# Down products of a transformer block by seven matrix products instead of eight, with three row operands kept in DRAM

## The chip, the core and the metric

The kernel runs on one core of a Trainium2 chip. The metric is the device time of one execution in microseconds (us). The core has five engines that run their own queues of instructions in order and wait for each other through semaphores: TensorE (PE, matrix products into PSUM), VectorE (DVE), ScalarE (ACT), GpSimd (POOL) and SyncE (SP, which here issues DMA transfers).

## The reference

The reference is one transformer block on 2048 rows of width 576 in float32: layer norm, attention with 32 heads, a residual, then a second layer norm and a gated feed-forward with 4608 inner columns.

```python
x = A_x
h = x + _A_ref(_layernorm(x), A_wqkv, A_wo)          # attention
def _B_ref(x, w_gate, w_up, w_down):
    g = einsum("bsd,df->bsf", x, w_gate)
    u = einsum("bsd,df->bsf", x, w_up)
    return einsum("bsf,fd->bsd", gelu(g) * u, w_down)
h2 = h + _B_ref(_layernorm(h), B_w_gate, B_w_up, B_w_down)
```

The change lies in the last product, gelu(g) * u times w_down, called the down product here.

## The kernel before

Matrices are cut into a high and a low float16 part, and a product is made of high-high, high-low and low-high parts, three matmuls where one float32 product would be one.

The feed-forward runs over 18 chunks of 256 inner columns. Two chunks make a super chunk (nine of them, the loop over `sc`, L1289). The rows lie in two halves of 1024 (`p` = 0 and 1), each of two blocks of 512. For a chunk and a half, `unit(c, p)` (L1051) makes gate and up products by a Strassen scheme of Winograd's form: seven products for gate and seven for up, in turn, each of seven matmuls of 128x512 (L1065) that accumulate in a bank. There are six banks, g[0..2] for gate and u[0..2] for up. The operands of the rows are 35 pieces (five for each of B22, B11, B21, T1, T2, T3, T4); 18 of each half lie in the region X and 17 in the region V. After each product, elementwise work follows: ACT copies a bank (`copy`), DVE adds another bank to the copy, ACT takes the gelu (L1070), DVE multiplies by the up value (`gate`, L1073), ACT writes the high float16 part of the result (`high`, L1076) and POOL the low part (`low`, L1079). A unit gives four blocks of h: two row blocks by two column blocks of 128.

After the two chunks of a super chunk, `down(p)` (L1142) makes the down product for that half: for 8 row tiles of 128 and 2 column halves of 288, twelve matmuls of 128x288 (L300) into one of four banks in turn, and then one DVE instruction (L1155) that adds the bank, scaled, into the rows `nat`. So a down has 16 groups of 12 matmuls.

The order in a super chunk is: unit(c, 1), unit(c+1, 1), down(1), unit(c+2, 0), unit(c+3, 0), down(0), where the last three belong to the next super chunk. The order on PE, ACT, DVE, POOL and SP is that of the program text. Beside the main work runs `side`, a chain of generators that cuts the next chunks' weights: one step of it is taken after each product of a unit and each group of a down (`beside`, L1265). `split_matrix` (L927) has steps for sums of weight blocks on POOL (L936), maxima on DVE (L129), a transpose on PE, a run of six tiny DVE instructions (L142 to L173) that make the scale, and then three highs on ACT (L952: one of 1152 columns, two of 768) and three lows on DVE (L966 and L968). `split_down` (L1021) cuts the down weights in the same way, with four highs and four lows of 576 columns. Weights come by DMA on SP's queue into one buffer in the region A.

Of the lines in the listing below, the prediction's steps use `unit`, `down`, `split_matrix`, `split_down` and the loop over `sc`.

## Time and profile before

| what | before |
|---|---|
| median of 3 runs | 2670.18 us (2669.16 to 2671.85) |
| the profiled execution's own time | 2668.08 us |
| its span, first to last instruction | 2666.3 us |
| mean granted TensorE clock | 0.996 of full speed |
| first matmul of the feed-forward (L1065) | at 1449.2 us of the span |
| PE busy, whole span | 97% |
| DVE busy, whole span | 76% |
| ACT, POOL busy | 61%, 29% |

The page gives busy time, a span in 40 slices, DMA queues, the chain of work that ended last, and groups of instructions by line. A wait is shown as idle time of the engine ahead of an instruction, with what released it. In the timeline each row has start, duration, engine, line, and in brackets the idle time before it.

### The profile page before, as it was taken

How to read it: one execution, taken by the hardware profiler on the slowest of the kernel's cores; microseconds unless marked ns; L12 is line 12 of the kernel's file. 1: busy time of each engine (PE TensorE's matmuls, PEld its weight loads, DVE VectorE, ACT ScalarE, POOL GpSimd, SP SyncE). 2: the span in 40 equal slices, each digit the busy share in tenths (PEclk: the TensorE clock that was granted, in tenths of full speed). 3: DMA queues.
4: the chain of work that ended last, by engine and by line, in shares of the span. 5: the costliest groups of instructions: out<-in, count | busy, mean ns of one | idle time of the engine just before them, and what ended most of it. 6: DMA issues, size and time to landing. Idle time of an engine off the chain costs nothing.

```text
span 2666.3 us, 44517 instructions
## 1 busy us (share of the span) xinstructions
PE 2589.7 (97%) x16665; PEld 1118.6 (42%) x16665; DVE 2013.1 (76%) x3872; ACT 1619.2 (61%) x2128; POOL 777.3 (29%) x1040
## 2 busy tenths in 40 slices
PE   6999999999999999999999899999999999999999
PEld 2542222222222222222243555555555555555555
DVE  6367999999999999999967866566666666666653
ACT  5215999999999999999956433333333333333332
POOL 2200352132223232221666532222222222222221
PEclk9999999999999999999999999999999999999999
DMA  8411101010101010110116321010101010101010
GB/s 222 94 40 51 54 26 30 19 42 15 42 14 45 17 42 19 30 25 20 36 47 125 74 51 40 23 40 23 40 22 40 24 39 25 38 27 36 29 59 36
DMA packets 171466, 114.70 MB, mean 43 GB/s; under 512 B 90872, under 2 KB 149772, under 8 KB 171250
## 3 DMA queue, kind: packets, MB, share of 16 engines
q1 hardware_dynamic: 163566, 99.06, 13.9%
q0 software_dynamic: 7552, 12.79, 1.8%
q8 instruction: 130, 2.13, 0.3%
q14 instruction: 86, 0.70, 0.1%
q10 hardware_dynamic: 132, 0.01, 0.0%
HBM read 76.51 MB, written 15.01 MB: 34 GB/s over the span
## 4 chain that ended last, share of the span: by engine, by line
PE 67%; ACT 15%; issue 7%; DVE 4%; POOL 2%; DMA 2%; SPq 0%; ACTq 0%; DVEq 0%; POOLq 0%
PE more L1065 14%; PE bank L1065 13%; ACT WK L644 10%; PE bank L300 10%; PE bank L648 9%; PE more L300 8%; PE bank L589 7%; PE pair L300 4%; ACT nat L595 4%; PE pair L642 2%; DVE mx L601 1%; DMA nat<-rc 1%; ACT nat L662 0%; POOL A L996 0%; DMA V<-V 0%
## 5 line engine op out<-in xcount | busy, mean ns | idle before, releaser
L644 ACT ACTIVATE WK<-pair 128x1024 f32<-128x1024 f32 x1024 | 1000.0, 1041 | 84.8 <-PE pair L642 84.1
L601 DVE TENSOR_REDUCE mx<-bank 128x1 f32<-128x512 f32 x1552 | 975.7, 683 | 42.8 <-PE bank L589 32.4
L648 PE MATMUL bank<-WK,V 128*32 128x512 f32 x4096 | 547.7, 606 | 0.2 <-ACT nat L662 0.2
L300 PEld LDWEIGHTS <-WK 128*128 128x128 f16 x3456 | 338.0, 98 | 90.9 <-ACT WK L1076 1.7
L1065 PEld LDWEIGHTS <-W 128*128 128x128 f16 x2394 | 234.3, 98 | 282.9 <-issue 5.7
L589 PE MATMUL bank<-W 54*128 54x512 f16 x896 | 258.2, 379 | 14.0 <-DVE mx L601 1.8
L589 PE MATMUL bank<-A 54*128 54x512 f16 x904 | 255.0, 380 | 16.8 <-DVE mx L601 5.3
L671 POOL TENSOR_TENSOR rp<-rc,minus_one 128x16 f32<-128x16 f32 x28 | 81.9, 2926 | 537.1 <-DMA rc<-nat 537.1
L300 PE MATMUL more<-W,WK 128*128 128x288 f16 x1728 | 235.6, 286 | 2.2 <-ACT WK L1076 1.4
L300 PE MATMUL bank<-W,WK 128*128 128x288 f16 x1728 | 235.2, 286 | 0.0
L1065 PE MATMUL bank<-X,W 128*128 128x512 f16 x792 | 223.8, 379 | 0.0
L642 PE MATMUL pair<-A 56*128 56x512 f16 x1024 | 212.9, 381 | 2.3 <-ACT WK L644 1.4
L642 PE MATMUL pair<-W 56*128 56x512 f16 x1024 | 210.3, 380 | 4.3 <-ACT WK L644 3.2
L1065 PE MATMUL bank<-V,W 128*128 128x512 f16 x720 | 202.4, 379 | 0.4 <-ACT tmp L1115 0.3
L936 POOL TENSOR_TENSOR A<-A 128x384 f32<-128x384 f32 x136 | 137.0, 1028 | 202.6 <-DMA A<-in_B_w_up_dram 118.7
L589 PEld LDWEIGHTS <-W 54*128 54x128 f16 x1024 | 75.1, 93 | 283.6 <-issue 266.6
L599 DVE CUSTOM_DVE_ANT_0 nat<-bank,nat 128x512 f32<-128x512 f32 x248 | 171.4, 691 | 27.1 <-PE pair L642 4.4
L589 PEld LDWEIGHTS <-A 54*128 54x128 f16 x1024 | 72.3, 93 | 267.9 <-issue 250.8
L1079 POOL TENSOR_TENSOR WK<-tmp,WK 128x512 f16<-128x512 f32 x73 | 87.9, 1203 | 305.9 <-ACT WK L1076 305.6
L1083 ACT COPY tmp<-more 128x512 f32<-128x512 f32 x36 | 21.0, 583 | 236.8 <-PE more L1065 198.2
L595 ACT ACTIVATE nat<-bank 128x512 f32<-128x512 f32 x248 | 151.4, 611 | 11.5 <-PE bank L589 11.5
L648 PEld LDWEIGHTS bank<-WK,V 128*32 128x32 f32 x4096 | 81.1, 108 | 179.0 <-issue 164.2
(304 smaller groups left out, 3259.9 us busy)
## 6 DMA issues: line engine op xcount, KB each, us to landing
A<-in_B_w_down_dram SPq DMA_DIRECT2D x8, 1152.0 KB
nat<-rc SPq DMA_DIRECT2D x32, 256.0 KB
A<-in_B_w_gate_dram SPq DMA_DIRECT2D x64, 128.0 KB
A<-in_B_w_up_dram SPq DMA_DIRECT2D x64, 128.0 KB
qk_hi<-tmp SPq DMA_DIRECT2D x36, 128.0 KB
qk_lo<-tmp SPq DMA_DIRECT2D x36, 128.0 KB
out_dram<-nat SPq DMA_DIRECT2D x16, 288.0 KB
X<-nat SPq DMA_DIRECT2D x100, 36.0 KB
```

The lines of the kernel that those rows point to most:

```text
L300: nc.tensor.matmul(dst, a, b, start=(i == 0), stop=(i == len(pairs) - 1))
L589: nc.tensor.matmul(pm[:, :TB], Q[r, q0 : q0 + P], keys, start=True, stop=True)
L595: nc.scalar.activation(row, pm[:, :TB], AF.Relu)
L599: nc.vector.tensor_tensor_reduce(row, pm[:, :TB], row, 1.0, LOWEST, ALU.add, ALU.max, dst)
L601: nc.vector.tensor_reduce(dst, pm[:, :TB], axis=AX.X, op=ALU.max)
L642: nc.tensor.matmul(pS[:, j, :TB], K[r, kt * P : (kt + 1) * P], Q[r, qc * TB : (qc + 1) * TB], start=True, stop=True)
L644: nc.scalar.activation(pes[(2 * kt + pr) % NPE], pS[:, :, :TB], AF.Exp, scale=ex_reg)
L648: nc.tensor.matmul(acc[32 * hh : 32 * hh + 32, :TB], Vg[n // NB][:, kt * G4 + hh * VC : kt * G4 + hh * VC + 32], pes[(2 * kt + hh // 2) % ...
L671: nc.gpsimd.tensor_tensor(rc, den, minus_one.to_broadcast([P, R]), op=ALU.pow)
L936: op(W8[:, d], W8[:, a], W8[:, b])
L1065: nc.tensor.matmul(bank, w, x_, start=start and i == 0, stop=i == len(mm) - 1, skip_group_check=not start)
L1079: nc.gpsimd.tensor_sub(hl[:, 2 * i + j], v, hh[:, 2 * i + j])
```

## The change

From the second super chunk on, the down product is made by the same Winograd form of Strassen's scheme: the four blocks of h and the four blocks of the down weights are combined into seven pairs, so `down7` runs 2 x 7 x 2 = 28 groups of six matmuls of 128x288, 168 in place of 192, and each group is followed by one DVE addition into `nat` (28 in place of 16). One bank may be accumulated into again by a later product after DVE has read it, as `b0` is by groups 1, 3, 5 and 7 of a pass, where a group now stands for two tiles i.

`unit7` takes the place of `unit` from chunk 2 on. It makes the products in another order (the pair S4 B22 ahead of A22 T4), and forms H1 to H4 from the four blocks of h. That makes four more DVE instructions with both inputs in SBUF (L1185, L1192, L1198, L1204), seven highs in place of four on ACT (L1130) and seven lows in place of four on POOL (L1133).

`split_down7` makes the seven combinations of the down weights: eight POOL instructions of 128x288, four highs (864, 1152, 864, 1152 columns) on ACT and four lows of the same sizes on DVE.

The larger buffers for h take the space of the pieces of the second half of the rows. So T2, T3 and T4 of both halves (15 pieces, 128x7680 float16) are written once to DRAM (`keep_pieces`, two transfers of 1.97 MB on ACT's queue), and from then on fetched into one place in V before they are needed (`fetch_pieces`: three transfers of 128x2560 float16, 655 KB, for each change of p, on SP's queue, issued in the unit that used that place last, `used`).

```diff
-    V = const.tile([P, 9936], F32, name="V")
+    V = const.tile([P, 10224], F32, name="V")
...
+    xs = [dram.tile([P, 15, TB], F16, name=f"xs{i}") for i in range(2)]
+
+    def piece(p, k, c):
 
         if k < 18:
             o = (2 * p + k // 9) * TB
             return XT[:, k % 9, o : o + TB]
-        return VP[:, p * PIECES + k - 18]
+        return VP[:, (p * PIECES if k < 20 or c < 2 else 0) + k - 18]
+
+    def keep_pieces(p):
+        nc.scalar.dma_start(xs[p], VP[:, p * PIECES + 2 : (p + 1) * PIECES])
+
+    def fetch_pieces(p, o):
+        nc.sync.dma_start(VP[:, 2 + 5 * o : 7 + 5 * o], xs[p][:, 5 * o : 5 * o + 5])
...
+    D11, D3, D21, D22, D1, D2, D4 = range(7)
+    dh7 = view(W, 23296, (2, 7, HALF), F16)
+    dl7 = [view(W, 31360, (7, HALF), F16), view(V, 36864, (7, HALF), F16)]
+    hts7 = [[view(r, o + 14 * TB * k, (7, TB), F16) for k in range(2)] for r, o in ((WK, 0), (V, 19456))]
...
+    def split_down7(sc):
+
+        raw = view(A, DS + 3 * 4 * HALF, (4, D))
+        T1, T2, T4 = (view(A, DS + 4 * HALF * i, (HALF,)) for i in range(3))
+        t124 = view(A, DS, (3, HALF))
+        ed = yield from exponents([raw[:, 2 * i : 2 * i + 2].rearrange("p a b -> p (a b)").unsqueeze(1)
+                                   for i in range(2)], "dn")
+        E = small.tile([P, 2], I32, tag="E", name="E")
+        nc.vector.tensor_add(E, ee[:, 0], ee[:, 1])
+        nc.vector.tensor_add(ed, ed, E)
+        M = small.tile([P, 1], I32, tag="M", name="M")
+        nc.vector.tensor_max(M, ed[:, 0:1], ed[:, 1:2])
+        nc.vector.tensor_sub(E, E, M.to_broadcast([P, 2]))
+        nc.vector.tensor_scalar(E, E, 1, 266, op0=ALU.mult, op1=ALU.add)
+        nc.vector.tensor_scalar_max(E, E, 0)
+        s = pow2(E, 1, 0, "s_dn")
+        dscs.append(pow2(M, 1, -259, "dsc"))
+
+        def sums(k):
+            B11, B12, B21, B22 = (raw[:, 2 * k + i // 2, i % 2 * HALF : (i % 2 + 1) * HALF] for i in range(4))
+            nc.gpsimd.tensor_sub(T1, B12, B11)
+            nc.gpsimd.tensor_sub(T2, B22, T1)
+            nc.gpsimd.tensor_sub(T4, B21, T2)
+            nc.gpsimd.tensor_sub(B12, B22, B12)
...
+        def high(j):
+            k, sl, src = jobs[j]
+            nc.scalar.activation(dh7[:, k, sl], src, AF.Copy, scale=s[:, k : k + 1])
+
+        def low(j):
+            k, sl, src = jobs[j]
+            nc.vector.scalar_tensor_tensor(dl7[k][:, sl], src, s[:, k : k + 1], dh7[:, k, sl],
+                                           op0=ALU.mult, op1=ALU.subtract)
+
+        sums(0)
+        yield
+        high(0)
+        yield
+        low(0)
+        high(1)
+        sums(1)
+        yield
+        low(1)
+        high(2)
+        yield
+        low(2)
+        high(3)
+        yield
+        low(3)
+        yield
+        blank_rows()
...
+    def unit7(product, gelu, gate, g, u, hh, hl, used):
...
+        xg, xu = next(tmp_ring), next(tmp_ring)
+        product(0, g[0], A11, B11, True)
+        nc.scalar.copy(xg, g[0])
+        yield
+        product(1, u[0], A11, B11, True)
+        nc.scalar.copy(xu, u[0])
+        yield
+        product(0, g[1], A12, B21, True)
+        nc.vector.tensor_add(xg, g[1], xg)
+        yield
+        product(1, u[1], A12, B21, True)
+        gelu(xg, xg)
+        nc.vector.tensor_add(xu, u[1], xu)
+        gate(xg, xu)
+        yield
+        ag, au = next(tmp_ring), next(tmp_ring)
+        product(0, g[0], S2, T2, False)
+        nc.scalar.copy(ag, g[0])
+        high(H11, xg)
+        yield
+        product(1, u[0], S2, T2, False)
+        used(0)
+        nc.scalar.copy(au, u[0])
+        low(H11, xg)
+        yield
+        bg, bu = next(tmp_ring), next(tmp_ring)
+        product(0, g[2], S1, T1, True)
+        nc.scalar.copy(bg, g[2])
+        yield
+        product(1, u[2], S1, T1, True)
+        nc.scalar.copy(bu, u[2])
+        yield
+        product(0, g[0], S3, T3, False)
+        nc.vector.tensor_add(bg, g[0], bg)
+        yield
+        product(1, u[0], S3, T3, False)
+        used(1)
+        gelu(bg, bg)
+        nc.vector.tensor_add(bu, u[0], bu)
+        gate(bg, bu)
+        yield
+        product(0, g[2], S4, B22, False)
+        nc.vector.tensor_add(ag, g[2], ag)
+        high(H22, bg)
+        gelu(ag, ag)
+        yield
+        product(1, u[2], S4, B22, False)
+        low(H22, bg)
+        nc.vector.tensor_add(au, u[2], au)
+        gate(ag, au)
+        nc.vector.tensor_add(xu, ag, bg)
+        yield
+        ga = next(tmp_ring)
+        product(0, g[0], A22, T4, False)
+        high(H1, xu)
+        gelu(ga, g[0])
+        low(H1, xu)
+        nc.vector.tensor_sub(bu, xu, xg)
+        high(H2, bu)
+        low(H2, bu)
+        yield
+        product(1, u[0], A22, T4, False)
+        used(2)
+        nc.vector.tensor_sub(au, xg, ag)
+        gate(ga, u[0])
+        high(H12, ga)
+        low(H12, ga)
+        high(H3, au)
+        low(H3, au)
+        nc.vector.tensor_sub(bg, ga, bu)
+        high(H4, bg)
+        low(H4, bg)
...
+        if c >= 2:
+            yield from unit7(product, gelu, gate, g, u, hh7, hl7, used or (lambda o: None))
+            return
...
+    def down7(p, dsc, last):
+
+        b0, b1, b2 = ((banks[i], banks[i + 3]) for i in (1, 0, 2))
+
+        def product(i, bank, a, b, start):
+            tsl = slice(i * P, (i + 1) * P)
+            mm = []
+            for k in range(2):
+                hh, hl = (v[:, a, tsl] for v in hts7[k])
+                mm += [(hh, dh7[:, k, b]), (hh, dl7[k][:, b]), (hl, dh7[:, k, b])]
+            for n, (w, x_) in enumerate(mm):
+                nc.tensor.matmul(bank[:, :HALF], w, x_, start=start and n == 0, stop=n == len(mm) - 1,
+                                 skip_group_check=not start)
+
+        def add(i, bank, *outs):
+            for j, n in outs:
+                t = (2 * p + j) * TPB + i
+                ws = slice(n * HALF, (n + 1) * HALF)
+                nc.vector.scalar_tensor_tensor(nat[:, t, ws], bank[:, :HALF], dsc, nat[:, t, ws],
+                                               op0=ALU.mult, op1=ALU.add)
+
+        for i0 in (0, 2):
+            for bank, a, b, start, outs in ((b0, H11, D11, True, ((0, 0),)),
+                                            (b2, H1, D1, True, ((1, 1),)),
+                                            (b0, H2, D2, False, ((0, 1),)),
+                                            (b1, H12, D21, True, ((0, 0),)),
+                                            (b0, H3, D3, False, ((1, 1),)),
+                                            (b2, H4, D22, False, ((0, 1),)),
+                                            (b0, H22, D4, False, ((1, 0),))):
+                for i in range(2):
+                    product(i0 + i, bank[i], a, b, start)
+                    add(i0 + i, bank[i], *outs)
+                yield
+            if last:
+                for i in range(2):
+                    for j in range(2):
+                        t = (2 * p + j) * TPB + i0 + i
+                        nc.sync.dma_start(ov[:, t], nat[:, t])
+            b0, b1 = b1, b0
+        banks[:] = [banks[i] for i in (1, 0, 2, 4, 3, 5)]
...
-                      split_matrix(c + 3, 1, None, lambda sc=sc: load_down(sc + 1), 2))
-            dn = split_down(sc + 1)
+                      split_matrix(c + 3, 1, None, lambda sc=sc: load_down7(sc + 1), 2))
+            dn = split_down7(sc + 1)
             side = chain(until_ready(g2))
+        if sc == 0:
+            keep_pieces(0)
         beside(unit(c, 1), side, head=0 if sc else 7)
         run(side)
+        if sc == 0:
+            keep_pieces(1)
         if not last:
             side = chain(g2, pause(2), u2, pause(2), g3, pause(2), u3, pause(4), dn)
-        beside(islice(u := unit(c + 1, 1), 13), side)
+        beside(islice(u := unit(c + 1, 1, None if last else lambda o: fetch_pieces(0, o)), 13), side)
         run(u)
-        beside(down(1, dsc, last), side, head=2)
+        beside(down7(1, dsc, last) if sc else down(1, dsc, last), side, head=2)
         if last:
             break
+        if sc == 0:
+            tmps[5] = view(WK, 14336, (TB,))
         run(u2)
         beside(unit(c + 2, 0), side)
         run(u3)
-        beside(unit(c + 3, 0), side)
+        beside(unit(c + 3, 0, lambda o: fetch_pieces(1, o)), side)
         run(dn)
         if sc + 2 < NCH // 2:
             load_matrix(w_gate, c + 4)
-        beside(down(0, dscs[-1], sc == NCH // 2 - 2), iter(()))
+        beside(down7(0, dscs[-1], sc == NCH // 2 - 2), iter(()))
     in_order.close()
 
 
```

Three places show how the rows stand. The first is DVE's queue at the end of the second unit of p = 1, ahead of down(1). Before (L1132 and L1136 add banks, L966 and L968 are lows of the next up weights, L1073 is the gate, L1155 the first additions of the down):

```order
L1132 TENSOR_TENSOR WK<-more_12981,WK 128x512
L966 SCALAR_TENSOR_TENSOR WK<-A,p_s_m_20846,W 128x768
L968 SCALAR_TENSOR_TENSOR W<-A,p_s_m_20846,W 32x3x128
L1136 TENSOR_TENSOR W<-bank_68,W 128x512
L1073 SCALAR_TENSOR_TENSOR WK<-W,p_hsc_20014,WK 128x512
L1155 SCALAR_TENSOR_TENSOR nat<-more_12979,p_dsc,nat 128x288
L1155 SCALAR_TENSOR_TENSOR nat<-bank_66,p_dsc,nat 128x288
L1155 SCALAR_TENSOR_TENSOR nat<-more_12980,p_dsc,nat 128x288
```

Now (L1183 adds a bank, L1185, L1192, L1198 and L1204 are the new sums, L978 and L980 the lows, L1342 the additions of the down; six tiny instructions that end in L173 are shown by the last one):

```order
L1183 TENSOR_TENSOR WK<-bank_68,WK 128x512
L1232 SCALAR_TENSOR_TENSOR WK<-WK,p_hsc_17880 128x512
L1185 TENSOR_TENSOR V<-WK,A 128x512
...
L173 TENSOR_SCALAR p_s_m_18728<-pi_s_m_18726 128x1
L1192 TENSOR_TENSOR tmp_81<-V,tmp_81 128x512
L978 SCALAR_TENSOR_TENSOR WK<-A,p_s_m_18728,W 128x768
L980 SCALAR_TENSOR_TENSOR W<-A,p_s_m_18728,W 32x3x128
L1198 TENSOR_TENSOR WK<-tmp_81,WK 128x512
L1232 SCALAR_TENSOR_TENSOR tmp_81<-bank_67,p_hsc_17880,tmp_81 128x512
L1204 TENSOR_TENSOR A<-tmp_81 128x512
L1342 SCALAR_TENSOR_TENSOR nat<-more_12981,p_dsc,nat 128x288
L1342 SCALAR_TENSOR_TENSOR nat<-bank_66,p_dsc,nat 128x288
```

The tiny instructions, which stood before the last bank additions, and four new sums now stand between the bank addition L1183 and the first addition of the down.

The second is ACT's queue at the end of the first unit of p = 0, ahead of the second. Before (L952 highs of weights, L1111 and L1115 copies, L1070 gelu, L1076 highs of h, L1083 the first copy of the next unit):

```order
L952 ACTIVATE W<-A,p_s_m_18971 128x1152
L952 ACTIVATE W<-A,p_s_m_18971 128x768
L1111 COPY A<-more_12979 128x512
L952 ACTIVATE W<-A,p_s_m_18971 128x768
L1115 COPY tmp_81<-bank_66 128x512
L1070 ACTIVATE A<-A,p_gsc_18515 128x512
L1070 ACTIVATE tmp_81<-more_12979,p_gsc_18515 128x512
L1076 CAST WK<-A 128x512
L1076 CAST WK<-tmp_81 128x512
L1070 ACTIVATE WK<-WK,p_gsc_18515 128x512
L1076 CAST WK<-WK 128x512
L1083 COPY tmp_81<-more_12979 128x512
```

Now (L964 highs of weights, L1229 gelu, L1130 highs of h; the gelu that reads the bank `more_12981` is the last of the four):

```order
L964 ACTIVATE W<-A,p_s_m_19112 128x1152
L1229 ACTIVATE A<-A,p_gsc_18638 128x512
L964 ACTIVATE W<-A,p_s_m_19112 128x768
L1130 CAST WK<-A 128x512
L1229 ACTIVATE WK<-WK,p_gsc_18638 128x512
L964 ACTIVATE W<-A,p_s_m_19112 128x768
L1130 CAST WK<-V 128x512
L1229 ACTIVATE tmp_81<-more_12981,p_gsc_18638 128x512
L1130 CAST WK<-tmp_81 128x512 x2
L1130 CAST WK<-WK 128x512
L1130 CAST WK<-A 128x512
L1137 COPY tmp_81<-more_12981 128x512
```

The highs of the weights moved in between the gelus, and the gelu that reads the bank of g[0] now comes behind a high of a new sum (L1130 WK<-V).

The third is DVE's queue at the end of the second unit of p = 0, ahead of down(0). Before (L1041 lows of the down weights):

```order
L1073 SCALAR_TENSOR_TENSOR A<-tmp_81,p_hsc_20014,A 128x512
L1041 SCALAR_TENSOR_TENSOR W<-A,p_s_dn,W 128x576
L1073 SCALAR_TENSOR_TENSOR tmp_81<-bank_66,p_hsc_20014,tmp_81 128x512
L1132 TENSOR_TENSOR WK<-more_12981,WK 128x512
L1136 TENSOR_TENSOR W<-bank_68,W 128x512
L1073 SCALAR_TENSOR_TENSOR WK<-W,p_hsc_20014,WK 128x512
L1155 SCALAR_TENSOR_TENSOR nat<-more_12979,p_dsc,nat 128x288
L1155 SCALAR_TENSOR_TENSOR nat<-bank_66,p_dsc,nat 128x288
```

Now (L1100 lows of the down weights, L1177 and L1183 bank additions):

```order
L1177 TENSOR_TENSOR WK<-more_12983,WK 128x512
L1100 SCALAR_TENSOR_TENSOR W<-A,p_s_dn,W 128x1152
L1183 TENSOR_TENSOR WK<-bank_68,WK 128x512
L1232 SCALAR_TENSOR_TENSOR WK<-WK,p_hsc_19032 128x512
L1185 TENSOR_TENSOR V<-WK,A 128x512
L1100 SCALAR_TENSOR_TENSOR V<-A,p_s_dn,W 128x864
L1192 TENSOR_TENSOR tmp_81<-V,tmp_81 128x512
L1100 SCALAR_TENSOR_TENSOR V<-A,p_s_dn,W 128x1152
L1198 TENSOR_TENSOR WK<-tmp_81,WK 128x512
L1232 SCALAR_TENSOR_TENSOR tmp_81<-bank_66,p_hsc_19032,tmp_81 128x512
L1204 TENSOR_TENSOR A<-tmp_81 128x512
L1342 SCALAR_TENSOR_TENSOR nat<-more_12982,p_dsc,nat 128x288
```

Before, the last low stood ahead of the last two bank additions (L1132, L1136). Now two of the four lows, each of half as many columns again or twice as many, stand behind the last one (L1183), among the new sums.

21 lines of the change are left out of this document (17 added, 4 removed).

## The prediction

> **What bounds the kernel now.** I read the chain of waits first, in a window that holds a whole super chunk, then the stages, then the timelines of DVE, ACT and POOL at the ends of units.
>
> ```profile
> PE 2589.7 (97%) x16665; PEld 1118.6 (42%) x16665; DVE 2013.1 (76%) x3872; ACT 1619.2 (61%) x2128; POOL 777.3 (29%) x1040
> ...
> 1909.95 1.51 PE bank L1065 x7
> 1911.46 1.47 PE more L300 x12
> ...
> 1933.51 1.47 PE bank L300 x12
> 1934.98 1.51 PE more L1065 x7
> ...
> 1977.51 1.47 PE more L300 x12
> ...
> 1911.46:1934.98 23.52, 23.52 (x194) 18.75 (x192) 9.13 (x17) 0.62 (x1) 5.39 (x6) 1.00 0.08 24
> 1911.46:2043.77 132.31, 132.31 (x785) 76.78 (x783) 82.71 (x160) 48.38 (x72) 35.90 (x34) 1.00 0.11 32
> ```
>
> Through units and downs the chain is PE alone, without a gap: a product of a unit takes 1.51 us, twelve matmuls of a down 1.47, a down 16 x 1.47 = 23.52 (first window row), a super chunk 132.31 (second). After the core's own time stand busy PE, PEld, DVE, ACT, POOL: DVE has 82.71 of 132.31. So removed matmuls are worth their full time, but only while the other engines deliver at the ends of units.
>
> **What is removed.** A down has 168 matmuls in place of 192: 24 x 1.47 / 12 = 2.94 us. Sixteen downs are changed (p = 1 of super chunks 2 to 9, p = 0 the same): 47.0 us off PE.
>
> **What is added.** Per super chunk DVE gets 24 more additions and 16 sums, ACT and POOL twelve highs and lows and the wider cuts of the down weights. In total that fits: 24 x 0.44 + 16 x 0.60 + about 2 = 22 us on DVE, 105 of 126. It doesn't fit where it falls. These rows give the prices (start, duration, line):
>
> ```profile
> 1911.50 0.69 DVE L1136 TENSOR_TENSOR W<-bank,W 128x512 f32<-128x512 f32 x1 [0.82 <-PE bank L1065]
> 1912.30 0.75 DVE L1073 SCALAR_TENSOR_TENSOR WK<-W,p_hsc,WK 128x512 f32<-128x512 f32 x1
> 1912.97 0.52 DVE L1155 SCALAR_TENSOR_TENSOR nat<-more,p_dsc,nat 128x288 f32<-128x288 f32 x1
> ...
> 1975.26 0.28 DVE L142 TENSOR_REDUCE ab_m<-bank 128x1 f32<-128x128 f32 x1
> ...
> 1976.27 0.68 DVE L1132 TENSOR_TENSOR WK<-more,WK 128x512 f32<-128x512 f32 x1
> 1977.68 1.02 DVE L966 SCALAR_TENSOR_TENSOR WK<-A,p_s_m,W 128x768 f16<-128x768 f32 x1 [0.73 <-ACT W L952]
> 1978.73 0.61 DVE L968 SCALAR_TENSOR_TENSOR W<-A,p_s_m,W 32x384 f16<-32x384 f32 x1
> 1979.37 0.69 DVE L1136 TENSOR_TENSOR W<-bank,W 128x512 f32<-128x512 f32 x1
> ...
> 1980.83 0.51 DVE L1155 SCALAR_TENSOR_TENSOR nat<-more,p_dsc,nat 128x288 f32<-128x288 f32 x1
> 1981.26 0.51 DVE L1155 SCALAR_TENSOR_TENSOR nat<-bank,p_dsc,nat 128x288 f32<-128x288 f32 x1
> ...
> 1984.31 0.74 DVE L966 SCALAR_TENSOR_TENSOR WK<-A,p_s_m,W 128x512 f16<-128x512 f32 x1
> 1985.07 0.48 DVE L968 SCALAR_TENSOR_TENSOR W<-A,p_s_m,W 32x256 f16<-32x256 f32 x1
> ...
> 2030.36 0.42 DVE L142 TENSOR_REDUCE ab_dn<-more 128x2 f32<-128x256 f32 x1
> ...
> 2033.43 0.17 DVE L173 TENSOR_SCALAR p_s_dn<-pi_s_dn 128x2 int32<-128x2 int32 x1
> ...
> 1976.39 1.26 ACT L952 ACTIVATE W<-A,p_s_m 128x1152 f16<-128x1152 f32 x1 [0.39 <-DVE p_s_m L173]
> 1977.55 0.71 ACT L1070 ACTIVATE WK<-WK,p_gsc 128x512 f32<-128x512 f32 x1
> ...
> 1980.95 0.62 ACT L1076 CAST WK<-WK 128x512 f16<-128x512 f32 x1 [1.86 <-DVE WK L1073]
> 1981.47 0.93 ACT L952 ACTIVATE W<-A,p_s_m 128x768 f16<-128x768 f32 x1
> ```
>
> From start to start: an addition whose result the next needs 0.80, otherwise 0.60 (0.69 less the same overlap as 0.75 to 0.67); a gate 0.67, or 0.86 if its result is needed (0.75 and the 0.11 of the pair above); a down addition 0.43; a low of 768 with its tail 1.05 + 0.64, of 512 0.76 + 0.50; the six tiny instructions 1.01, and ACT's high of 1152 starts 1.13 after the first of them and takes 1.26; a high of h 0.62, the next on ACT 0.52 after its start. The tiny instructions of the down weights take 3.24 to their scale. A sum with both inputs in SBUF is not in these rows: between the addition (0.69) and the gate (0.75), I take 0.69, since it is an addition. Lows of 864 and 1152: 1.12 and 1.43, on the line through 512 and 768 (between 1.02 and twice 0.74).
>
> In each place below t = 0 is when PE would end the fourteenth product undisturbed; product 12 then ends at -3.02, 9 at -7.55.
>
> Place one, unit to unit of p = 1, 8 times. The old unit ended with products on g[2] and u[2], which the next unit needs seventh. The new one ends on g[0] and u[0], which the next unit needs first. On DVE: au add -2.98, gate -2.18, the new sum -1.32 to -0.63; then ACT's high of it and behind that, in order, the gelu that empties g[0]: -0.06 to 0.63 (0.69 as an addition from a bank). PE waits 0.7 us.
>
> Place two, unit to unit of p = 0, 8 times. ACT's order is the second one shown. The tiny instructions start at -6.91, so the 1152 runs from -5.78 to -4.52; the gelu behind it ends at -3.90, and DVE's gate starts at -3.85. Behind the gate stand, in order: low 768 (-3.18), addition (-1.49), low 512 (-0.89), addition (0.38), gate (1.18), sum (2.04 to 2.73); ACT's high, and the gelu that empties g[0], to 3.99. Then u[0] comes free 0.4 late too. PE waits 4.4 us.
>
> Place three, second unit of p = 1 into its down, 7 times (the last has no side work). Sum -1.32, tiny instructions -0.72, ACT's 1152 to 1.67, low 768 at 1.74, then sum, gate, sum, and the first down addition at 5.49 to 6.01. The third group, on the same bank as the first, was due at 2 x 1.47 = 2.94: PE waits 3.1. Before, four banks in turn left that addition 4.4 us, and it was late too (1980.83, with the down's first matmul at 1977.51), at no cost.
>
> Place four, second unit of p = 0 into its down, 8 times. The 3.24 us put the first addition at -7.1 and the gate at -5.2. Then low 864 (-4.53), addition, low 1152 (-2.88), addition (-1.52), gate, sum (0.14), low 864 (0.74), sum, low 1152 (2.39), sum (3.75), gate, sum, and the first down addition, 5.81 to 6.33. PE waits 3.4; the first group alone waits until 3.8 for the last low. POOL's second four sums for these weights (0.88 each, an estimate on the line given below) follow the first low 864 and end at 0.1, just in time for ACT's last two highs.
>
> Together 8 x 0.7 + 8 x 4.4 + 7 x 3.1 + 8 x 3.4 = 89.7 us: the lower end, engines undisturbed.
>
> **DVE and POOL exclude each other.** The lows of h on POOL now crowd at these ends, beside DVE instructions with two SBUF inputs.
>
> ```profile
> 1972.80 1.55 DVE L1073 SCALAR_TENSOR_TENSOR A<-tmp,p_hsc,A 128x512 f32<-128x512 f32 x1
> ...
> 1982.39 0.96 DVE L966 SCALAR_TENSOR_TENSOR WK<-A,p_s_m,W 128x512 f16<-128x512 f32 x1
> ...
> 1969.81 3.99 POOL L936 TENSOR_TENSOR A<-A 128x384 f32<-128x384 f32 x4 [2.38 <-DMA A<-in_B_w_up_dram]
> ...
> 1981.64 1.16 POOL L1079 TENSOR_TENSOR WK<-WK 128x512 f16<-128x512 f32 x1 [4.29 <-ACT WK L1076]
> ```
>
> The gate met the last POOL addition (to 1973.80) and took 0.80 longer than 0.75; the low 512 met a POOL low (to 1982.80) and took 0.22 longer than 0.74. In both the work began some 0.2 before POOL's end. Put into the places with 1.16 for a POOL low and 0.88 for one of 288 columns (on the line of 512 at 1.16 and 384 at 3.99 / 4): place two has two such meetings, +1.6; place three two, +1.6; place four five, +3.7. Place one can go either way, 0. That is 8 x 1.6 + 7 x 1.6 + 8 x 3.7 = 53.6 more at full meeting, 0 at none. I take three quarters, 40, since which of the two is first is not settled by the order.
>
> The Trainium skill, "SBUF — State Buffer", section "SBUF: two separate sides", states that the port pair shared by DVE and GpSimd is an exclusive lock held for the whole instruction. The rows agree in kind and are 0.2 us per meeting milder; by the page nine meetings a super chunk would add another 0.2 each, some 14 us.
>
> **Transfers.** Six fetches of 0.655 MB are added to a window that moves 0.11 of the DMA capacity: 0.22, hidden. Each is issued behind the last use of its place, and a down and some twelve products lie between that and its next use: 14 x 1.47 + 12 x 1.51 = 38.7 us. On SP's queue it stands behind or ahead of weight loads; if the cover were gone, PE would wait for one transfer per change of p, about 4 us (0.655 MB at the 178 GB/s of the output's transfers below are 3.7), 16 x 4 = 64. The two writes to DRAM lie in the first super chunk. At the end, four tiles are sent out together in place of one:
>
> ```profile
> core 0: 2666.3 us, clock 0.996
> ...
> 2662.35 0.52 DVE L1155 SCALAR_TENSOR_TENSOR nat<-bank,p_dsc,nat 128x288 f32<-128x288 f32 x1 [0.95 <-PE bank L300]
> ...
> GB/s 0 0 5 0 0 0 0 0 0 0 0 0 0 0 10 0 0 0 0 0 0 0 0 0 0 0 178 75 113 164 14 178 0 178 36 142 125 53 178 0
> ```
>
> The last tile now takes 2666.3 - 2662.9 = 3.4 us; two more at 0.3 MB behind it cost 0 to 3.4, I take 2.5.
>
> **The sum.** The profiled execution took 2668.1 (span 2666.3 and 1.8 around it), 2.1 under the median. 2668.1 - 47.0 + 89.7 + 40 + 2.5 = 2753; as a median 2755. Ends: no meetings 2715, all of them 2769.
>
> **Rivals.** (1) Faster: PE's own work decides, as it did in every super chunk before. 2668.1 - 47.0 + 2.5 + 2.1 = 2626. For it speaks the unbroken chain; against it, that the trace has a place where DVE is full, and PE waits there at once:
>
> ```profile
> 1500.00:1505.00 5.00, 4.50 (x20) 1.81 (x19) 5.00 (x8) 5.00 (x10) 2.22 (x2) 1.00 0.22 42
> ...
> 1508.69 1.67 PE L1065 MATMUL more<-X,W 128*128 128x512 f16 x7 [1.64 <-DVE W L1112]
> ```
>
> It decides if the waits per super chunk stay under 5.9 us, half of the 11.2 (89.7 / 8) above. (2) Waits without meetings: 2715. (3) The clock falls in the waits. The trace has two idle stretches of PE that were followed by half speed:
>
> ```profile
> 54.00:56.00 2.00, 0.00 (x0) 0.00 (x0) 0.00 (x0) 2.00 (x7) 0.00 (x0) 0.50 1.21 219
> ...
> 72.00:76.00 4.00, 0.13 (x2) 0.00 (x0) 3.63 (x13) 1.93 (x5) 0.41 (x1) 1.00 0.35 114
> 76.00:80.00 4.00, 3.55 (x19) 2.40 (x19) 1.08 (x1) 1.18 (x5) 2.62 (x4) 0.66 0.41 76
> ```
>
> After some 4.3 idle us the granted clock was 0.66 over 4 us, a loss of 0.34 x 4 = 1.4. Places two and four are near that length: 16 x 1.4 = 22, so 2777. The Trainium skill, "TensorE: Matmul & The Clock Gate", part 1, gives an idle window of about 3.4 us for this; the rows agree. (4) A wait on the fetches: 2626 + 64 = 2690. Against it stand the 38.7 us of cover.
>
> **Chances.** Waits with meetings (2730 to 2770) 0.52; without (2700 to 2730) 0.19; clock too 0.11; fetches 0.03; faster 0.11; within 0.2%, which a measurement can't tell from none, 0.04. So faster 0.11, same 0.04, slower 0.85. The range 2695 to 2810 leaves out faster, same and a few hundredths at each end.
>
> **What would show it.** Right: PE idle ahead of L1224 on ACT's gelu (L1229) of 4 us or more eight times, ahead of L1335 on DVE (L1342, L1100) of 3 us and more fifteen times, super chunks near 143 us, sums (L1192, L1198) that take longer than 0.69 on the mean. Wrong: super chunks of 126 to 132 us with no PE wait at these four places, or waits on the fetched pieces (L793).

## The result, and the profile after

The changed kernel takes 2815.59 us (median of 4 runs, 2813.07 to 2816.01), the kernel before 2671.01 beside it (4 runs, 2669.16 to 2672.09): a ratio of 1.054, 95% interval 1.0522 to 1.0558. The forecast was 2755, 2695 to 2810. The direction is right, the time lies 5.6 us above the range.

The page of the changed kernel, busy time by engine, and the windows of a whole super chunk (from the end of place two to the next) and of two stretches behind waits; the columns are those of the prediction's windows, ending in granted clock, DMA share and GB/s:

```profile
PE 2606.0 (93%) x16281; PEld 1099.4 (39%) x16281; DVE 2263.1 (80%) x4192; ACT 1678.7 (60%) x2224; POOL 979.5 (35%) x1200
...
1781.70:1933.00 151.30, 133.22 (x735) 73.72 (x735) 114.35 (x201) 55.97 (x84) 61.04 (x54) 0.94 0.18 54
...
1781.70:1783.70 2.00, 2.00 (x5) 0.69 (x5) 2.00 (x3) 0.54 (x1) 0.88 (x1) 0.50 0.43 56
...
1887.00:1889.00 2.00, 2.00 (x10) 1.27 (x9) 1.57 (x4) 1.08 (x2) 2.00 (x3) 0.50 0.46 135
```

A super chunk takes 151.3 us where 132.3 were before, and where 132.31 - 2 x 2.94 = 126.4 would be PE's own work. PE is idle for 18.1 of it, and its matmuls take 133.2 - 126.4 = 6.8 longer: the clock is 0.94 in the mean and 0.50 behind the places. The same over the whole span: PE's busy time without the removed matmuls would be 2589.7 - 47.0 = 2542.7 and is 2606.0, so 63.3 us longer, most of it slower matmuls; its idle time was 2666.3 - 2589.7 = 76.6 and is 2813.4 - 2606.0 = 207.4, so 130.8 more. 130.8 + 63.3 - 47.0 = 147.1 is the difference of the two spans.

PE's waits in the changed kernel, by line and releaser (us in total, times, longest), and one super chunk's of them in the timeline (start, duration, in brackets the wait and who ended it):

```profile
PE more L1224 <- ACT tmp L1229: 40.1, 16, 4.8
PE more L1335 <- DVE V L1100: 28.9, 8, 3.8
PE more L1335 <- DVE nat L1342: 19.1, 8, 2.8
PE more L1335 <- ACT W L1096: 17.8, 7, 2.8
PE more L1335 <- ACT V L1130: 12.4, 8, 1.9
PE more L1335 <- POOL V L1133: 9.0, 8, 1.1
```

```profile
1808.05 0.28 PE L1335 MATMUL more<-W,V 128*128 128x288 f16 x1 [2.85 <-ACT W L1096]
1812.13 0.40 PE L1335 MATMUL more<-V 128*128 128x288 f16 x1 [3.79 <-DVE V L1100]
...
1855.95 1.67 PE L1224 MATMUL more<-X,W 128*128 128x512 f16 x7 [0.58 <-ACT tmp L1229]
...
1881.41 0.30 PE L1335 MATMUL more<-W,V 128*128 128x288 f16 x1 [1.84 <-ACT V L1130]
...
1882.97 0.30 PE L1335 MATMUL more<-W,V 128*128 128x288 f16 x1 [1.14 <-POOL V L1133]
...
1886.83 0.88 PE L1335 MATMUL more<-W,WK 128*128 128x288 f16 x3 [2.83 <-DVE nat L1342]
...
1933.00 3.14 PE L1224 MATMUL more<-X,W 128*128 128x512 f16 x7 [4.77 <-ACT tmp L1229]
```

All four places wait, and the six rows add up to 127.3 us. In order of time: place four 2.85 + 3.79, place one 0.58, place three 1.84 + 1.14 + 2.83, place two 4.77. The product behind place two takes 3.14 where the one behind place one takes 1.67. (A product's row is 1.67 long without a wait too: from start to start it is 1.51, and the row's last 0.16 lies beside the next product. Behind a wait those 0.16 are not shared, and count as busy.) Behind place three the clock fell too, though no single wait there is over 2.83.

Most of these rows name ACT, but ACT itself was held up. At place two it stood idle for 1.91 us until DVE's sum (L1185) was done, made the high of that sum, and then the gelu that PE waits for. At place four its high of the down weights had waited 2.36 us for POOL's sums of them (L1087), 19.7 us over the whole run.

DVE and POOL at place three of the changed kernel (timeline), and the means of two of the new sums, whose inputs both lie in SBUF (groups by shape, busy us, mean ns). The down at place three starts on PE at 1877.57:

```profile
1871.68 0.95 DVE L129 TENSOR_REDUCE ac_m<-A 128x1 f32<-128x768 f32 x1 [2.43 <-DMA A<-in_B_w_up_dram]
...
1877.85 0.69 DVE L1185 TENSOR_TENSOR V<-WK,A 128x512 f32<-128x512 f32 x1
...
1882.88 1.47 POOL L1133 TENSOR_TENSOR V<-tmp,V 128x512 f16<-128x512 f32 x1
1883.35 1.53 DVE L1198 TENSOR_TENSOR WK<-tmp,WK 128x512 f32<-128x512 f32 x1
```

```profile
L1192 DVE TENSOR_TENSOR tmp<-V,tmp 128x512 f32<-128x512 f32 x32 | 34.5, 1079 | 0.6
L1198 DVE TENSOR_TENSOR WK<-tmp,WK 128x512 f32<-128x512 f32 x32 | 34.5, 1077 | 0.2
```

A new sum beside a POOL low takes 1.53, and the two sums of the table take 1.08 on the mean and not 0.69. And DVE comes late to place three: the first new sum (L1185) starts 0.28 after the down's start, where the prediction's walk has -1.32. In its queue stand the maxima of the up weights (L129), which had waited 2.43 us for their DMA.

### The profile page after: what moved, and what is told of

It reads as the page before. It is cut to its first block, busy times and chain, and to the rows that moved or that the text cites. A ratio compares the mean times of both kernels' runs of the same rounds, so it can differ in the third digit from the quotient of the medians.

```text
span 2813.4 us, 44711 instructions
## 1 busy us (share of the span) xinstructions
PE 2606.0 (93%) x16281; PEld 1099.4 (39%) x16281; DVE 2263.1 (80%) x4192; ACT 1678.7 (60%) x2224; POOL 979.5 (35%) x1200
## 4 chain that ended last, share of the span: by engine, by line
PE 54%; ACT 18%; DVE 14%; issue 9%; DMA 3%; POOL 1%; SPq 1%; ACTq 0%; DVEq 0%; POOLq 0%
ACT WK L644 11%; PE bank L648 9%; PE more L1224 9%; PE bank L1224 8%; PE bank L589 7%; PE more L1335 6%; PE bank L1335 6%; ACT nat L595 4%; PE pair L300 4%; PE bank L300 3%; PE pair L642 2%; DVE WK L1232 1%; DVE W L980 1%; DMA A<-in_B_w_up_dram 1%; DVE mx L601 1%
## 5 line engine op out<-in xcount | busy, mean ns | idle before, releaser
L964 ACT ACTIVATE W<-A,p_s_m 128x768 f16<-128x768 f32 (+1 forms) x78 | 78.8, 1035 | 181.2 <-DVE p_s_m L173 181.2
L1335 PEld LDWEIGHTS <-V 128*128 128x128 f16 x1344 | 137.7, 103 | 117.4 <-issue 49.5
L1224 PE MATMUL more<-X,W 128*128 128x512 f16 x468 | 128.6, 404 | 42.9 <-ACT tmp L1229 40.1
L1335 PEld LDWEIGHTS <-WK 128*128 128x128 f16 x1344 | 139.2, 104 | 67.4 <-issue 22.0
L1335 PE MATMUL more<-W,V 128*128 128x288 f16 x448 | 128.8, 305 | 39.2 <-ACT W L1096 17.8
L595 ACT ACTIVATE nat<-bank 128x512 f32<-128x512 f32 x248 | 151.5, 611 | 10.6 <-PE bank L589 10.6
```

What stands on the lines that cost most here:

```text
L595: nc.scalar.activation(row, pm[:, :TB], AF.Relu)
L1224: nc.tensor.matmul(bank, w, x_, start=start and i == 0, stop=i == len(mm) - 1, skip_group_check=not start)
L1335: nc.tensor.matmul(bank[:, :HALF], w, x_, start=start and n == 0, stop=n == len(mm) - 1, skip_group_check=not start)
```

## The experiments

Each kernel is the changed one with the edit shown; each was timed beside the kernel before, which took 2670.65 to 2672.36 us. The expectations name the kernels by labels that begin with their number here (e7_all is kernel 7). Kernels 3, 4, 8, 10 and 12 leave out work that the result needs, so they price that work and are no versions to use. "The trace" of a kernel is one of its executions.

### 1. The waits filled with matmuls

```diff
+def warm(bank, n):
+    for _ in range(n):
+        nc.tensor.matmul(bank[:, :TB], id16, XT[:, 0, :TB], start=True, stop=True)
...
 run(u3)
+warm(banks[1], 18)
 beside(unit(c + 3, 0, lambda o: fetch_pieces(1, o)), side)
...
+warm(banks[1], 20)
 beside(down7(1, dsc, last) if sc else down(1, dsc, last), side, head=2)
...
+warm(banks[1], 25)
 beside(down7(0, dscs[-1], sc == NCH // 2 - 2), iter(()))
```

> The changed kernel, with matmuls that compute nothing of use put into three of the four waits: 18 of 128x512 ahead of the first product at place two (4.4 us of wait on the mean), 20 ahead of the down at place three (5.1), 25 at place four (5.8), each 0.216 us at full clock, into a bank that is free. Nothing else moves, so the other engines are as late as before. Theory (the half speed behind the waits is the clock, and it falls because PE stood idle): PE's busy time without the added 23 x 21 matmuls falls by the 63.3 us that it is over the old sum (2606.0 against 2589.7 - 47.0), the clock is 1.00 behind the places, and the time is 2815.6 - 63 = 2752, up to 10 more where the added matmuls overshoot a wait. Rival (the matmuls behind a wait are slow for another reason, such as weights and operands that are written at that moment): half speed stays, 2815 or more.

Measured: 2796.8 us, 1.0469 (1.045 to 1.0489). Its page, its waits, and a super chunk:

```profile
PE 2660.0 (95%) x16765; PEld 1129.9 (40%) x16765; DVE 2267.6 (81%) x4192; ACT 1678.2 (60%) x2224; POOL 978.6 (35%) x1200
...
PE more L1339 <- DVE nat L1346: 29.8, 21, 2.0
PE more L1224 <- ACT tmp L1229: 11.2, 15, 0.9
...
PE more L1339 <- DVE V L1100: 7.8, 7, 1.4
PE bank L1224 <- DVE tmp L1232: 7.5, 7, 1.1
...
1780.24:1930.48 150.24, 141.36 (x798) 78.04 (x797) 115.36 (x201) 55.93 (x84) 61.01 (x54) 1.00 0.17 54
...
1884.48 0.53 PE L1339 MATMUL more<-W,WK 128*128 128x288 f16 x3 [1.85 <-DVE nat L1346]
...
1889.25 1.45 DVE L978 SCALAR_TENSOR_TENSOR WK<-A,p_s_m,W 128x512 f16<-128x512 f32 x1
1890.71 1.11 DVE L980 SCALAR_TENSOR_TENSOR W<-A,p_s_m,W 32x256 f16<-32x256 f32 x1
...
1892.43 0.53 PE L1339 MATMUL more<-W,WK 128*128 128x288 f16 x3 [1.91 <-DVE nat L1346]
```

The clock stays at 1.00, so it was PE's idleness that lowered it. Of PE's busy time 484 x 0.216 = 104.5 is added work; without it 2555.5 are left, 50.5 less than in the changed kernel. But the time falls by 18.8 only. The waits, filled or not, are now 104.5 + 29.8 + 11.2 + 7.8 + 7.5 = 160.8, where they were 127.3. From the second changed super chunk on, the added work outlasts the wait at none of the three places: each is followed by one more. In the first, where the changed kernel waits only 1.77 at place two and 3.84 at place four, it does, by an estimated 3.7 us together (3.89 and 5.40 were put in). So more than half of what the slow matmuls took was time that PE would have waited anyway. The first expectation was right that the half speed is the clock, and wrong in what that costs: 19 us, not 63.

The last four rows are place three of one super chunk. With the clock up, PE waits there twice: once for the down's first additions, and once more for a later one, behind lows of the up weights that stand among the additions on DVE. In the changed kernel the slow matmuls cover the second wait.

### 2. Banks turned between the units of a stage

```diff
+def turn_banks():
+    banks[:] = [banks[i] for i in (1, 2, 0, 4, 5, 3)]
```

It is called behind unit(c, 1) and behind unit(c + 2, 0).

> The changed kernel with the banks turned between the two units that share a stage: the next unit starts on the bank that the third product has left free long ago, and meets the one that the late gelu empties only at its seventh product, 9 us later. Theory (places one and two wait for a bank, and only for that): the 40.1 us of PE waits on the gelu vanish, with them the clock's fall at place two (some 63.3 / 23 = 2.75 a place, 8 x 2.75 = 22), so 2815.6 - 62 = 2754; if DVE carries its 4.4 us of backlog on into place four, up to 20 of it comes back there: 2754 to 2775. Rival (DVE as a whole is what sets the pace, so a wait that is taken away comes back at the next place in full): 2800 to 2815.

Measured: 2800.38 us, 1.0475 (1.0458 to 1.0492), 15 less than the changed kernel, as the rival said. The waits on the gelu are gone; in their place stands

```profile
PE more L1224 <- ACT tmp L1137: 26.4, 7, 3.8
```

L1137 is ACT's copy of the next unit's first product, which the fifth product needs. It stands on ACT behind the last high (L1130), and that behind DVE's four sums. With the bank free at once PE meets the same backlog four products later.

### 3. Lows of h shortened on POOL

```diff
-nc.gpsimd.tensor_sub(hl[:, k], v, hh[:, k])
+nc.gpsimd.tensor_sub(hl[:, k, :64], v[:, :64], hh[:, k, :64])
```

> The changed kernel with each low of h on POOL made for 64 of its 512 columns (the rest of the lows is left out, so the down products miss part of h). POOL's 1.16 us each become about 0.25, and the instructions that DVE and POOL must do one after the other are nearly gone at the ends of units. Theory (exclusion, 1.6 at places two and three, 3.7 at four): 8 x 1.6 + 7 x 1.6 + 8 x 3.7 = 53.6 us of waits go, and part of the clock's falls with them, 0 to 40: 2720 to 2762; two-input sums on DVE go from a mean over 1 us back to 0.69. Rival (no exclusion; the places are DVE's queue alone, and only the 9.0 us that PE waits for POOL's lows go): 2800 to 2810.

Measured: 2764.71 us, 1.0349 (1.0332 to 1.0367), 50.9 less, 3 above the range of the theory. Groups by shape on DVE, and waits of PE:

```profile
L1192 DVE TENSOR_TENSOR tmp<-V,tmp 128x512 f32<-128x512 f32 x32 | 22.0, 687 | 0.6
L1198 DVE TENSOR_TENSOR WK<-tmp,WK 128x512 f32<-128x512 f32 x32 | 23.5, 734 | 0.2
```

```profile
PE more L1224 <- ACT tmp L1229: 34.1, 16, 4.0
PE more L1335 <- DVE nat L1342: 18.1, 12, 2.2
PE more L1335 <- ACT W L1096: 17.5, 7, 2.5
PE more L1335 <- DVE V L1100: 15.3, 8, 2.0
...
PE more L1335 <- ACT V L1130: 3.6, 8, 1.3
PE more L1335 <- POOL V L1133: 2.5, 8, 0.4
```

The sums are back at 0.69 and 0.73. The waits add up to 91.1, 36.2 less than with POOL's lows whole (6.5 of it waits for POOL itself); PE's busy time is 16.0 less (2590.0 for 2606.0), which is the rest of the gain. So exclusion costs some 30 to 36 us of waits, and the waits without it are 91, both with a clock that still falls (0.981 on the mean).

### 4. Without the sums of h

```diff
-nc.vector.tensor_add(xu, ag, bg)
...
-high(H1, xu)
-low(H1, xu)
-nc.vector.tensor_sub(bu, xu, xg)
-high(H2, bu)
-low(H2, bu)
...
```

> The changed kernel without the four sums of h, their highs on ACT and lows on POOL (the down products then read what lay there). All matmuls, the down additions, the wider split of the down weights, the fetches and the new order of banks stay. Theory (the crowding at the ends of units is what costs, and the 47.0 us off PE are real): places one and two fall to nothing, three and four keep what the down additions have of side work ahead of them, 1 to 2 us each without two of their sums: 2815.6's counterpart is 2670.2 - 47.0 + 2.5 + 15 x 1.5 = 2648, 2626 to 2660, faster than the kernel before. Rival (the transfers, the down additions or the wide splits cost as much as the sums do): over 2700.

Measured: 2711.51 us, 1.0151 (1.0134 to 1.0168): 104 less, but not the 2648 expected; it lies in the rival's range, over 2700. What is left:

```profile
PE more L1323 <- ACT W L1096: 18.6, 7, 3.0
PE more L1212 <- ACT tmp L1217: 15.6, 7, 2.2
PE more L1323 <- DVE V L1100: 14.2, 8, 2.6
```

The first and third are the down weights' split (place four), the second is the gelu behind ACT's high of 1152 columns (place two): side work, which this kernel still has at the same points. Whether that or the rival's down additions and transfers are to blame, kernels 10 and 12 decide.

### 5 to 7. Earlier side steps, another order at a unit's end, and both with turned banks

```diff
-beside(unit(c + 2, 0), side)
+beside(unit(c + 2, 0), side, more_at={5: 3})
-beside(unit(c + 3, 0, lambda o: fetch_pieces(1, o)), side)
+beside(unit(c + 3, 0, lambda o: fetch_pieces(1, o)), side, more_at={2: 3})
```

Here `more_at` gives the number of side steps at a product, where it isn't one.

> The changed kernel with the side steps of the p = 0 stage earlier: at one product in each of its two units three side steps are taken in place of one (the two empty ones behind the maxima), so that the up weights' lows end two products earlier (the last at product 10, not 12) and the down weights' lows four products earlier (at 8, not 12). Same instructions, same banks. Theory (what PE waits for at places two and four is side work ahead of the unit's own on DVE): 3.0 us less backlog at place two (4.4 us of wait on the mean, so 1.5 is left), 6 less at place four (5.8, so 0 to 1 is left); 8 x 3 + 8 x 5.3 = 66 us of waits less, some 10 of the clock more: 2735 to 2760. Rival (DVE has no room anywhere, so the order within a unit doesn't matter, as turning the banks gave only 15 us): 2790 or more.

Kernel 6 changes the first unit of a stage:

```diff
 product(0, g[0], A22, T4, False)
+gelu(ga, g[0])
 yield
 product(1, u[0], A22, T4, False)
+gate(ga, u[0])
+nc.vector.tensor_add(xu, ag, bg)
+high(H1, xu)
...
```

> The changed kernel with another order at the end of a stage's first unit (places one and two): the gelu that empties g[0] ahead of the new sums' highs on ACT, the gate that empties u[0] ahead of the four sums on DVE; the same instructions. Theory (as with the turned banks: the copy of the next unit's first product stands on ACT behind the last high, and that behind DVE's four sums, so what is freed at the first product is waited for at the fifth): the waits on the gelu fall from 40.1 to under 10 and come back by some 3.8 x 7 = 26 ahead of the fifth product: 2795 to 2810. Rival (the banks are all that place two waits for): 2815.6 - 8 x (4.4 + 2) = 2765.

Kernel 7 has the edits of kernels 2, 5 and 6.

> The three edits together: side steps of the p = 0 stage earlier, the other order at the end of a first unit, the banks turned between the units of a stage. Theory (backlog on DVE at the ends of units, and three orders that make PE meet it at once): places one and two cost nothing, place four 1 us, place three is as it was, 5.1 of wait and 2 of clock: 2626 + 8 x 1 + 8 x 7.1 = 2691, 2680 to 2715. Rival (DVE is the bound over the whole super chunk): over 2740.

Measured: earlier steps 2768.37 us, 1.0367 (1.035 to 1.0384), 47 less, 8 above the range of its theory; the other order 2813.82, 1.0534 (1.0516 to 1.0551), which the noise doesn't tell from the changed kernel and which neither expectation has; all three 2794.21, 1.0467 (1.0449 to 1.0485), so 26 more than the earlier steps alone, as the rival said. With the other order the waits on the gelu fell to 15.6 us, but PE's idle time is 208.7 where it was 207.4: 11.0 now stand at PE's transposes of the weights' maxima (L138), 7.1 at the copies ahead of the fifth product, the rest elsewhere. PE's waits with the earlier steps, then with all three:

```profile
PE more L1224 <- ACT tmp L1229: 19.3, 16, 2.0
...
PE bank L1224 <- ACT tmp L1165: 15.5, 7, 2.3
```

```profile
PE bank L138 <- DVE am_dn L133: 14.6, 4, 3.9
PE more L138 <- DVE am_dn L133: 14.2, 4, 3.5
```

With earlier steps the waits on the down weights' split (28.9 + 17.8) are gone and the gelu's halved, but 25 us come back at ACT's copies (L1165) and, 10.0 of them, at the transposes. With all three edits places one and two no longer hold PE up, and DVE's backlog reaches the transposes, which stand in PE's own queue: 28.8 us. A wait that is taken away at one place lets PE run into the next.

### 8. Without the fetches

```diff
-nc.sync.dma_start(VP[:, 2 + 5 * o : 7 + 5 * o], xs[p][:, 5 * o : 5 * o + 5])
```

> The changed kernel without the 45 fetches of kept pieces from DRAM (the third operands are then those of other rows from the third super chunk on). Theory (the fetches are hidden): 2815, within 5 either way. Rival (they hold up the weight loads on SP's queue, whose landing DVE waits for by 20 us in the profile, and so the side steps): 2780 to 2800.

Measured: 2805.03 us, 1.0498 (1.0481 to 1.0516), 10.6 less, between the two expectations. In the changed kernel PE never waits for a fetched piece. DVE's waits for the up weights, ahead of their maxima, are 25.3 us with the fetches and 19.8 without. But that trace is the slowest of kernel 8's four executions (2811.63 us; the others took 2802.68 to 2805.04), and PE's idle time in it is 207.4 us, the same as in the changed kernel. So the trace doesn't show where the 10 us come from, and that later weights cost them is not shown.

### 9, 11 and 13. Side steps spread further

Kernel 9 is kernel 7 with other steps; 11 is kernel 5 with the up weights' first low behind the down's first additions; 13 is 11 with an empty step ahead of the down weights' first high.

```diff
-beside(islice(u := unit(c + 1, 1, None if last else lambda o: fetch_pieces(0, o)), 13), side)
+beside(islice(u := unit(c + 1, 1, None if last else lambda o: fetch_pieces(0, o)), 13), side, more_at={12: 0})
-beside(down7(1, dsc, last) if sc else down(1, dsc, last), side, head=2)
+beside(down7(1, dsc, last) if sc else down(1, dsc, last), side, head=2, more_at={10: 2})
```

In unit(c + 2, 0) the steps are {6: 2} in kernel 9 and {5: 2, 6: 2} in 11 and 13; in unit(c + 3, 0) they are {0: 2, 10: 2}, {2: 3} and {2: 3, 4: 0}.

> The three edits of e7_all, with the side steps placed otherwise: the maxima of the down weights get their room back (PE's transposes of them waited 28.8 us in e7_all), the up weights' first low of the p = 1 stage stands behind the down's first additions and not ahead of them (place three), the later steps catch up by one double step each. Theory (backlog on DVE at the ends of units, met because of order): places one and two nothing, place three 2 us for its 5.1, place four 1.5, the waits on maxima gone, a clock that falls at most at place three: 2626 + 8 x (2 + 1.5 + 1.5) = 2666, 2655 to 2715. Rival (DVE, at 114 of the 126.4 us that PE's work takes in a super chunk, has too little room, so a backlog that isn't waited for at one place is carried to the next): over 2740.

> e5_early, and in the p = 1 stage the up weights' first low two steps later, behind the down's first additions (place three); banks and the units' own order as in the changed kernel. Theory (the low and its tail, 1.7 us and a meeting with POOL, are ahead of the down's first addition): 2 to 3 us less at place three, and the clock's fall there is milder: 2768 - 8 x 3.5 = 2740, 2730 to 2755. Rival (what goes from ahead of the additions comes back among them, in the down): 2760 or more.

> e11_early_late with one empty step between the down weights' scale and ACT's first high of them, so that POOL's four sums are done when ACT comes to it; there PE waited 14.2 + 3.8 us for ACT's copies of the unit's own behind that high. The down weights' lows end at product 9 and not 8. Theory: those 18 us go and nothing comes back before place four: 2752 - 18 = 2734, 2725 to 2745. Rival (DVE carries it on): 2748 or more.

Measured: 2781.34 (1.0409, 1.0391 to 1.0426), 2751.76 (1.0297, 1.0279 to 1.0314), 2756.03 (1.0321, 1.0301 to 1.0342). Kernel 9 and kernel 13 went as their rivals said; kernel 11, in its range, is the fastest version that leaves nothing out, 64 us under the changed kernel and 81 over the one before (kernel 13 is not told from it by the noise). In kernel 13 the 18 us of waits on L1165 and L1157 went as planned, and waits on highs (L1130) rose from 16.0 to 26.5: carried on.

### 10 and 12. The floor

Kernel 10 is kernel 4 with the steps of kernel 5; kernel 12 is kernel 4 with the short lows of kernel 3 and the steps of kernel 11, but {2: 2, 4: 0} in unit(c + 3, 0).

> e4_no_sums (without the four sums of h, their highs and lows) with the earlier side steps of e5_early. Theory (the 47.0 us off PE are real, and come out as soon as DVE has no backlog at the ends of units): the 18.6 + 14.2 us of waits on the down weights' split and the 15.6 on the gelu of e4_no_sums go, with the clock's falls behind them; 2626 is the floor, 2630 to 2655 expected, faster than before. Rival (something else in the change costs: the 28 additions of a down, the fetches): 2690 or more.

> Without the four sums of h, their highs and lows, and with the other lows of h on POOL 64 columns wide (both left out of what the down products read), the side steps as in e11_early_late but the down weights' own with room for their maxima (PE's transposes waited 9.7 us on them in e10_early_no_sums) and for POOL's sums ahead of ACT's first high. All matmuls, the 28 additions of a down, the wide splits and the fetches stay. Theory (the 47.0 us off PE are real and only the backlog on DVE, with POOL's part in it, eats them): 2626 plus 10 to 25 of what is left at place three: 2635 to 2655, faster than the kernel before. Rival (the additions of the downs, 12 more each, or the fetches cost on their own): 2665 or more.

Measured: 2675.43 us, 1.0017 (1.0007 to 1.0026), for kernel 10, 20 above its range and under its rival's; 2646.11, 0.9915 (0.9889 to 0.994), in its range, for kernel 12. Kernel 12's page and the longest of its waits at the four places:

```profile
PE 2551.9 (96%) x16281; PEld 1081.5 (41%) x16281; DVE 2101.2 (79%) x4064; ACT 1611.8 (61%) x2096; POOL 714.4 (27%) x1072
...
PE more L1323 <- DVE V L1100: 8.5, 7, 1.2
```

With all 28 additions of a down, the wide splits and the fetches in place, the kernel is 25 us faster than the one before, under 1% but clear of the noise. So what eats the removed matmuls is not those, but the work that kernel 12 leaves out or moves: the four sums with their highs and lows, POOL's lows beside DVE, and the side steps at the ends of units. How the sums' part divides among DVE, ACT and POOL no run separates; the rows above show ACT waiting for DVE and POOL.

## Why the prediction was wrong, by its steps

**What bounds the kernel, what is removed.** Right. PE was the bound, and the removed matmuls are worth their time: with the waits nearly gone (kernel 12) the time is under the one before by 25 us, 20 above the 2626 of rival (1). PE's busy time there is 2551.9, so 37.8 less than before. The 9.2 missing from 47.0 and the waits that are left (the largest kind 8.5) make up about the 20.

**The four places.** Right in place and in kind, and PE's rows are those named, L1229 and L1335. Without exclusion the sum was 89.7; kernel 3 has 91.1. Exclusion at three quarters was 40; kernel 3 took away 36.2. Together 129.7 against 127.3. By place, taken and measured in the super chunk shown: one 0.7 and 0.58; two 5.6 (4.4 and three quarters of 1.6) and 4.77; three 4.3 and 5.81; four 6.2 and 6.64. At place three the wait has three parts, on a high of h, a low of h and the first addition, where the prediction saw only the last. That the totals agree is in part luck: the walk was made for a PE at full clock, and with the clock up (kernel 1) the waits are 160.8. In the changed kernel, and in kernel 3, slow matmuls cover some of them.

**The steps that failed: the clock, and place three.** The measured time is 60.6 above the 2755.

The sum had no term for the clock. It stood in rival (3), with a chance of 0.11, at 16 falls of 1.4 us, 22 in all. Of the 63.3 us by which PE's busy time is too long, 50.5 went in kernel 1 with the clock's falls, some 2.2 for each of the 23 times that PE comes to places two, three and four; at place two one product alone took 3.14 - 1.67 = 1.5 longer. The 1.4 came from one stretch of before with a mean of 0.66 over 4 us. What the prediction held against it, that only places two and four were long enough, didn't hold: place three is made of three shorter waits. The time, though, fell by only 18.8 in kernel 1, since the waits grew. That this is near rival (3)'s 22 is luck too, as that counted fewer and shorter falls and nothing to cover.

The larger part is in the waits: at full clock 160.8 where the sum had 129.7. With kernel 1's added matmuls and the waits behind them, places two, three and four take 5.8, 7.7 and 7.4 on the mean from the second changed super chunk on, where 5.6, 4.3 and 6.2 were taken. So place three makes up 7 x 3.4 = 24 of the 31. The walk had two things wrong there. It took DVE as free when the last bank addition came due, but DVE was 1.2 behind (L1183 starts 1.75 ahead of the down's start, not 2.98) and its gate before the sums met a POOL low; with the two meetings further on, the first addition of the down ends 9.2 after the start and not 6.0, or 7.6 with two full meetings. And it took that addition for the end of the backlog, where a second wait of 1.6 to 2.0 follows behind the up weights' later lows.

The rest is what PE's busy time is over the old sum even with the clock up, 2555.5 - 2542.7 = 12.8, of which the 0.16 behind each wait is a part. Less 1.3 at the end of the kernel, 18.8 + 31.1 + 12.8 - 1.3 = 61.4 accounts for the 60.6. Adding the 63.3 alone to the sum also gives 2818, near the 2815.6, but only because what the slow matmuls cover (33.5) is about what the walk had missed (31.1).

**Chances.** Waits on fetched pieces, rival (4), did not come, but without the fetches the time is 10.6 us less (kernel 8; by what path is open), where the prediction had them hidden. DVE is busy for 114.35 us of a super chunk where 105 were summed up, which leaves it less room than the prediction saw. The end of the kernel: from the last addition to the end 2813.4 - 2808.8 = 4.6 us against 3.4, so 1.2 for the 2.5 taken.

**What would show it.** Of the waits of 4 us and more on L1229, named eight times, seven came (4.8 each; the first of the eight is 1.77). Of the fifteen of 3 us and more on DVE ahead of L1335, seven came, at place four (3.8 on L1100); at place three none is over 2.83, as three waits make up the place. Super chunks near 143 us: 151.3, with matmuls 6.8 slower. The two sums took longer than 0.69, as named.

**Exclusion and the idle gap.** Two-input sums took 1.08 with POOL's lows whole and 0.69 and 0.73 with them short, so DVE and POOL do hold each other up. The Trainium skill, "SBUF — State Buffer", section "SBUF: two separate sides", with its exclusive lock for the whole instruction, would have added 14 us to full meeting; what kernel 3 took away, 36 of waits, lies under the full 53.6 already. Whether some lows met nothing, or slow matmuls covered part, isn't separated. The Trainium skill, "TensorE: Matmul & The Clock Gate", part 1, gives an idle window of some 3.4 us: kernel 11, below, shows falls behind waits of 1.2 us at most each, so here the length of one gap is no guide.

## What to carry to other kernels

Where PE waits at the end of a stage, and its clock falls with its idleness, a wait is to be priced with the slow work behind it, once for each place and not only for the longest wait. That price is not a saving to be had: here 50.5 us of slow work were worth 18.8, since the slow work covers backlog that would be waited for otherwise. So walk the queues at full clock, start the walk where the engine is known to be idle, and follow it past the first thing that is late.

In this kernel a backlog on DVE was met again wherever PE next needed DVE's results: freeing the bank that is waited for gave 15 us and reordering the unit's end nothing clear of the noise, while taking side steps earlier, where DVE had room, gave 47, and shortening POOL's lows 51. A scheme that trades matmuls for additions is to be judged at the point where the additions fall, not by the share of busy time of the engine that makes them.
